# VectorE's order around the second group of scores, in an attention and MoE kernel on one core

## The chip, the cores and the metric

The kernel runs on one core of a Trainium2 chip. The metric is the device time of one execution in microseconds (us), and less is better. The engines are TensorE (PE, with its weight loads as PEld), VectorE (DVE), ScalarE (ACT), GpSimd (POOL) and SyncE (SP), which only issues transfers here.

## What is computed

The attention has B, H, S, D = 4, 8, 576, 64. Its output goes through a feed-forward layer of 512 by 2048, over 2304 tokens. All is float32.

```python
scores = q @ k^T / 8, causal mask, softmax            # per batch and head
local  = softmax @ v
mem    = (phi(q) @ M_prev) / (phi(q) @ z_prev + 1e-6) # phi(x) = max(x, 0) + min(exp(x), 1)
x      = g * mem + (1 - g) * local                    # g = sigmoid(beta), one per head
h      = x @ w_in
out    = (h * sigmoid(1.702 h)) @ w_out
```

## The kernel before

Two heads form a pair. There are 16 pairs, four per batch. Batch 0 goes another way (`plan_rest`) and is not touched. The twelve pairs of batches 1 to 3 are laid out by `plan_full`; here they are called pair 1 to pair 12. Beside them TensorE works off the first feed-forward layer, 1536 matmuls into `pm` (float32 split into high and low words, 12 matmuls to a block of 128 outputs). They serve as filling: `feed` and `step` put them between the pairs' own matmuls, and those that are left when the last pair is done run alone. Then 1008 matmuls into `acc` form the second layer.

A pair's 576 queries are four row blocks of 128, i = 0 to 3, and a tail of 64. A row block goes through five steps: scores on TensorE, maximum on VectorE (`max_unit`, line 649), exponential on ScalarE (`exp_unit`, L657), sum and reciprocal on VectorE (`inv_unit`, L745 and L746), scaling on GpSimd (`scale_unit`, L660). Then VectorE transposes it in 32 by 32 blocks into `eT` (`a_blocks`, L874). The tail does the same, and its blocks are set by `t_blocks` (L884). Beside that stand the memory term's steps: GpSimd's `qp` and `qmt` (L578, L169), VectorE's `norm` (L594 and L599, sum over `qmt` and its reciprocal), GpSimd's product of `qp` and `nrm`, and VectorE's `qblocks` (L617).

TensorE's stations in a pair are these: the second group (`second_group`), the scores of row blocks 2, 1 and 0 into the banks `rows`; `pm` matmuls; the next pair's tail scores and the first part of the values (`early_values`: 16 products `po<-qpt` and 36 `po<-eT`, which need the blocks of tail, third rows i = 3 and row block 2); `pm` matmuls; the second part (47 products, row block 1); the next pair's third-row scores; the third part (45 products, row block 0); `pm` matmuls. The banks of `rows` are those of `po`, so the next second group waits until `x_sums` and `x_rests` (ACT `xh`, DVE `xl`) have read the values.

VectorE also decodes a 64-bit-stored weight matrix in most pairs (`bit_ops`, L1124, L1125 and L1127, here called the raw words), after ScalarE's scaling of it (L1142). ScalarE empties the `pm` banks (`hk`, L161); there are two of them in this stage.

What sets the order: each step is entered with a slot and a priority (`at(slot, prio, fn)`). Within an engine a scheduler orders what is emitted, by priority and by its own picture of time. `tc.add_manual_dep` pins two instructions: NOSYNC fixes an order on one engine, SYNC makes one wait for another. `group` gives a run of matmuls one common wait at its first instruction, and TensorE works strictly in its order.

Of the kernel before, what the change touches and what calls it, by code (L numbers as in the profile page):

```python
# [12 lines left out]
ALU = mybir.AluOpType  # L13
# [27 lines left out]
def tile_attention_memory_moe(ctx, tc, kq, vq, mem, vt, qt, mt, zz, beta, w_in, w_out, out):  # L41
# [3 lines left out]
    STEP = 7  # L45
    PACE = ((36, 1.97), (67, 1.95), (9999, 2.3))
    LATE = 4
# [488 lines left out]
    def plan_prep(p):  # L536
# [54 lines left out]
        def norm():  # L591
            n = sml.tile([128, 9, 1], F32, name="nrm", bufs=2)
            P["n"] = n
            x = nc.vector.tensor_reduce(out=n[:, X:, 0], in_=qmt[:, X:9], op=ALU.add, axis=AX.X)  # L594
            if rest:
                behind_x(x)
            elif "tr" in state:
                tc.add_manual_dep(x.ins, state["max"], NOSYNC, reason="not yet")
            state["norm"] = nc.vector.reciprocal(out=n[:, X:], in_=n[:, X:]).ins.name  # L599
# [103 lines left out]

    def alone(p):
        names = rooms(KEEP)
        prep[p]["tail"] = [bank("ps") for _ in range(2)]
        group([lambda: s_tail(p, prep[p]["tail"])], names)
# [5 lines left out]
    def row_steps(p, U):  # L713
# [3 lines left out]
        def max_unit(h, i):  # L717
            n = 128 * (i + 1)
            U["nm", h, i] = softmax_max([(U["ps", h, i][:, :n], n, mask[:, 512 - n:])])
            state["max"] = last_max[0]  # L720
            if "qblocks" in P:
                tc.add_manual_dep(first_max[0], P["qblocks"], NOSYNC, reason="not yet")

# [19 lines left out]
        def inv_unit(i):  # L743
            sm = U["rs", i] = sml.tile([128, 2], F32, name="sm")
            nc.vector.tensor_reduce(out=sm, in_=U["sm", i], op=ALU.add, axis=AX.X)  # L745
            state["inv"] = nc.vector.reciprocal(out=sm, in_=sm).ins.name  # L746

# [113 lines left out]
    def plan_full(p):  # L861
# [19 lines left out]
        def t_blocks():  # L881
            e, a = blocks(), P["at"].rearrange("p (k n) -> p k n", n=32)
            for o, src in ((e[:, :, 4], a[:, :16]), (e[:, 4:6, 0], a[:, 16:])):
                x = nc.vector.transpose(out=o, in_=src)  # L884
                behind_x(x)
                if ("tr", 3) in P:
                    tc.add_manual_dep(x.ins, P["tr", 3], NOSYNC, reason="not yet")
            P["tr", 4] = x.ins.name
# [67 lines left out]
        def early_values():  # L956
# [3 lines left out]
            if p + 1 < len(pairs):  # L960
                names += rooms(0)
                prep[p + 1]["tail"] = [bank("ps") for _ in range(2)]
                fns.append(lambda: s_tail(p + 1, prep[p + 1]["tail"]))
            room()
# [4 lines left out]
        def first_group():  # L969
# [5 lines left out]
            group(fns, names)  # L975
            U["from"] = state["pe"]

        def second_group():
# [13 lines left out]
        tail_steps(p, TURN - 6 if p == MB * NP else K0[p - 1] + 7)  # L992
        at(k0 + 4, 89.5, t_blocks)
        at(k0, 20, first_group)
        at(k0 + 3, 18, lambda: feed(U["from"] + 2.9 - state["pe"]))
        at(k0 + 3, 20, second_group)
        at(k0 + 3, 22, lambda: feed(1.0, True))
        for i, k in ((3, 0), (2, 3), (1, 3), (0, 3)):
            x = k0 + k + 1
            for h in range(2):  # L1000
                at(k0 + k + 1, 13 - i, lambda h=h, i=i: max_unit(h, i))
                at(x, (30, 29, 26, 25)[i], lambda h=h, i=i: exp_unit(h, i))
                at(x + 1, 13 - i, lambda h=h, i=i: scale_unit(h, i))
            at(x, 91 - i, lambda i=i: inv_unit(i))
            at(k0 + (4 if i == 3 else 6), (18, 17, 16, 89.4)[i], lambda i=i: a_blocks(i))
        at(k0 + 7, 40, early_values)
        at(k0 + 7, 99, lambda: feed(1.0, True))
        if p + 1 == len(pairs):
            at(k0 + 8, 30, flush)
        at(k0 + 8, 32, x_sums)  # L1010
# [443 lines left out]
```

## Time and profile before

| what | us |
|---|---|
| median of 3 runs | 598.63 (598.5 to 598.97) |
| profiled execution | 596.94 |
| its span, first to last instruction | 595.1 |
| TensorE matmul busy in the span | 550.7 (93%) |
| VectorE busy | 424.4 (71%) |
| ScalarE busy | 342.0 (57%) |
| GpSimd busy | 245.4 (41%) |

The profiled execution is 1.84 us longer than its span and 1.69 us shorter than the median. Pair 1 starts its second group at 101.29 us, pair 12 at 323.61 us; the values of pair 12 end at 342.73 us, 516 `pm` matmuls follow until 414.98 us, and then the second layer. TensorE is the engine to read; from 342.73 us on it hardly waits. [...]

### The profile page before, as it was taken

To read this page: it belongs to the slowest core of one execution; us is meant where nothing else is said; L and a number is where in the kernel's file an instruction comes from. 1 tells how busy PE (TensorE), PEld (TensorE's weight loads), DVE (VectorE), ACT (ScalarE), POOL (GpSimd) and SP (SyncE) were. 2 spreads that over 40 slices of the span, in tenths; PEclk is the share of its full clock that TensorE was granted. 3 is DMA by queue.
4 is the path that set the end of the run, shared out by engine and by line. 5 is a ranking of instruction groups with operands and counts; after the bars stand their busy time and mean duration, and the time that the engine had idled before them with its cause. 6 is when DMAs were issued, how large, how long until landed. Compare 5 with 4: busy or idle time off the path is not lost.

```text
span 595.1 us, 17373 instructions
## 1 busy us (share of the span) xinstructions
PE 550.7 (93%) x6984; PEld 493.8 (83%) x6984; DVE 424.4 (71%) x994; ACT 342.0 (57%) x815; POOL 245.4 (41%) x326
## 2 busy tenths in 40 slices
PE   5699998978979899999989699999999999999997
PEld 3367766866858788887877699999999999999997
DVE  5878776667686777877686466786596768667964
ACT  5778876555446455655554236555766865676441
POOL 4858557664576367446645412310413201320000
PEclk8599999989989899999999889999999999999999
DMA  7986444446447645674455655232734804560002
GB/s 236 381 275 211 148 131 137 152 162 228 170 133 243 209 152 184 227 236 155 160 182 167 211 169 158 89 123 94 271 92 153 266 22 134 180 216 4 28 0 80
DMA packets 48736, 97.73 MB, mean 164 GB/s; under 512 B 5520, under 2 KB 33424, under 8 KB 48656
## 3 DMA queue, kind: packets, MB, share of 16 engines
q1 hardware_dynamic: 42416, 74.60, 37.4%
q0 software_dynamic: 6240, 22.02, 12.0%
q8 instruction: 55, 0.90, 0.6%
q14 instruction: 25, 0.20, 0.1%
HBM read 73.01 MB, written 23.59 MB: 162 GB/s over the span
## 4 chain that ended last, share of the span: by engine, by line
PE 75%; ACT 9%; DVE 7%; POOL 4%; issue 4%; DMA 1%; ACTq 0%; POOLq 0%; DVEq 0%
PE acc L1296 30%; PE pm L142 27%; PE po L142 9%; PE ps L142 4%; ACT a L657 3%; PE rows L142 3%; DVE ps L649 2%; POOL qmt L169 1%; DVE eT L874 1%; ACT qmt L563 1%; DVE r L1125 1%; POOL a L660 1%; ACT at L657 1%; DMA vr<-in_vq_dram 1%; ACT hk L161 1%
## 5 line engine op out<-in xcount | busy, mean ns | idle before, releaser
L142 PE MATMUL pm<-xh,wi 128*128 128x320 f32 (+1 forms) x1024 | 215.1, 303 | 7.0 <-ACT hk L161 5.5
L142 PEld LDWEIGHTS pm<-xh,wi 128*128 128x128 f32 x1024 | 165.8, 191 | 15.8 <-ACT hk L161 6.6
L1296 PE MATMUL acc<-oh,wo 128*128 128x384 f32 x672 | 169.6, 336 | 0.0
L142 PE MATMUL pm<-xl,wi 128*128 128x256 f32 (+1 forms) x512 | 151.5, 296 | 0.0
L1296 PEld LDWEIGHTS acc<-oh,wo 128*128 128x128 f32 x672 | 121.9, 188 | 0.0
L1296 PE MATMUL acc<-ol,wo 128*128 128x384 f32 x336 | 111.2, 337 | 0.0
L660 POOL TENSOR_SCALAR a<-a,sm,g 128x512 f32<-128x512 f32 (+3 forms) x112 | 69.2, 629 | 99.9 <-DVE sm L746 60.6
L169 DVE TENSOR_TENSOR ol<-g,oh 128x768 fp32r<-128x768 f32 x84 | 79.6, 954 | 43.0 <-ACT oh L161 42.8
L142 PEld LDWEIGHTS pm<-xl,wi 128*128 128x128 f32 x512 | 97.6, 191 | 0.0
L161 ACT ACTIVATE oh<-g 128x768 fp32r<-128x768 f32 x84 | 69.8, 842 | 45.9 <-PE acc L1296 36.0
L1239 POOL DMA_DIRECT2D g<-gd x48 | 34.8, 729 | 115.0 <-DVE ol L169 61.8
L161 ACT ACTIVATE hk<-pm 128x256 f32<-128x256 f32 (+1 forms) x112 | 44.7, 407 | 47.1 <-PE pm L142 37.7
L142 PEld LDWEIGHTS po<-eT,vr 32*64 32x64 f32 x3072 | 51.7, 135 | 17.9 <-issue 11.5
L1296 PEld LDWEIGHTS acc<-ol,wo 128*128 128x128 f32 x336 | 62.9, 188 | 0.0
L142 PE MATMUL po<-eT,vr 32*64 32x32 f32 (+4 forms) x3072 | 55.9, 256 | 6.2 <-issue 6.1
L142 PE MATMUL ps<-kqf 64*64 64x512 f32 (+3 forms) x288 | 38.3, 544 | 12.5 <-ACT qmt L570 5.1
L1245 ACT ACTIVATE g<-g 128x768 f32<-128x768 f32 x48 | 39.4, 839 | 15.4 <-DMA g<-gd 15.4
L169 DVE TENSOR_TENSOR g<-g,g 128x768 f32<-128x768 f32 x48 | 45.4, 951 | 1.4 <-ACT g L1245 1.4
L657 ACT ACTIVATE a<-rows,nm 128x256 f32<-128x256 f32 (+2 forms) x72 | 33.2, 474 | 20.3 <-DVE nm L649 20.3
L649 DVE CUSTOM_DVE_ANT_0 ps<-ps,mask 128x512 f32<-128x512 f32 (+3 forms) x72 | 38.0, 555 | 8.5 <-PE ps L142 7.8
L874 DVE STREAM_TRANSPOSE eT<-a 128x1024 f32<-128x1024 f32 (+3 forms) x48 | 39.5, 830 | 3.1 <-POOL a L660 2.1
L161 ACT ACTIVATE xh<-po 128x256 fp32r<-128x256 f32 (+2 forms) x54 | 14.2, 311 | 47.7 <-PE po L142 46.9
(145 smaller groups left out, 758.0 us busy)
## 6 DMA issues: line engine op xcount, KB each, us to landing
g<-gd POOLq DMA_DIRECT2D x48, 384.0 KB, 4.6
vr<-in_vt_dram SPq DMA_DIRECT2D x24, 576.0 KB, 4.8
gd<-hk SPq DMA_DIRECT2D x64, 160.0 KB, 3.0
kqf<-in_kq_dram SPq DMA_DIRECT2D x12, 768.0 KB, 5.4
wraw<-in_w_in_dram SPq DMA_DIRECT2D x16, 512.0 KB, 5.7
gd<-hk SPq DMA_DIRECT2D x64, 128.0 KB, 2.6
wraw<-in_w_out_dram SPq DMA_DIRECT2D x10, 512.0 KB, 4.8
qr<-in_qt_dram SPq DMA_DIRECT2D x12, 288.0 KB, 3.0
```

The lines of the kernel that those rows point to most:

```text
L142: x = nc.tensor.matmul(out, l, r, start=start, stop=stop)
L161: return nc.scalar.activation(out=dst, in_=src, func=AF.Copy, **kw)
L169: return (nc.vector if eng == "V" else nc.gpsimd).tensor_tensor(out=dst, in0=a, in1=b, op=op)
L563: x = nc.scalar.activation(out=qm, in_=qv(), func=AF.Relu, scale=-1.0)
L649: x = nc.vector.tensor_tensor_reduce(out=ps, in0=ps, in1=mk, op0=ALU.add, op1=ALU.min, scale=-0.125, scalar=1e38 if j == 0 else nm[:, j - ...
L657: return nc.scalar.activation(out=a, in_=ps, func=AF.Exp, scale=-1.0, bias=nm, accum_out=sm)
L660: return (nc.vector if eng == "V" else nc.gpsimd).tensor_scalar(out=a, in0=a, scalar1=r, scalar2=gcol, op0=ALU.mult, op1=ALU.mult)
L874: x = nc.vector.transpose(out=blocks()[:, :4 * i + 4, i:9 - i:8 - 2 * i].rearrange("p k h n -> p h k n"), in_=U["a", i].rearrange("p h (k ...
L1125: nc.vector.scalar_tensor_tensor(out=si, in0=raw[:, :, 1], scalar=-2 ** 31, in1=si, op0=ALU.bitwise_and, op1=ALU.bitwise_or)
L1239: x = nc.gpsimd.dma_start(t, gd[4 * kh + p][:, :, t0:t0 + QN].rearrange("i p t -> p i t"))
L1245: x = nc.scalar.activation(out=t, in_=t, func=AF.Gelu_apprx_sigmoid)
L1296: nc.tensor.matmul(acc[b, j][:, :QN], W[2 * p + kk][:, WPART[i], sp, 128 * j:128 * j + 128], mv[:, kk], start=first and p + kk == 0 and sp ...
```

## The change

It leaves all arithmetic as it is and sets orders and waits.

- `norm` gets an order behind the maximum emitted last (the next pair's third rows). Before, a condition that never held kept that out.
- `t_blocks` moves from behind the third rows' blocks to a place behind `qblocks`, and the second group's first maximum is ordered behind it.
- The reciprocal of row block 2 (U["inv", 2]) stands ahead of the maxima of row block 0; the sums of row blocks 1 and 0 stand behind row block 2's transposition.
- The next pair's tail scores form a group of their own (`alone(p + 1, 0)`), with their own wait; the wait for the blocks moves to the first product `po<-qpt`.
- In the last pair the second and third part of the values get `pm` matmuls between them (`last_values`).
- `PACE` rises from 2.3 to 2.45 for the late slots, and `feed` after the second group asks for 0.2 instead of 1.0. That moves filling between places.

```diff
-    PACE = ((36, 1.97), (67, 1.95), (9999, 2.3))
+    PACE = ((36, 1.97), (67, 1.95), (9999, 2.45))
...
-            elif "tr" in state:
+            else:
                 tc.add_manual_dep(x.ins, state["max"], NOSYNC, reason="not yet")
...
-    def alone(p):
-        names = rooms(KEEP)
+    def alone(p, keep=KEEP):
+        names = rooms(keep)
...
-            if "qblocks" in P:
-                tc.add_manual_dep(first_max[0], P["qblocks"], NOSYNC, reason="not yet")
+            if ("tr", 4) in P:
+                tc.add_manual_dep(first_max[0], P["tr", 4], NOSYNC, reason="not yet")
+            if i == 0 and ("inv", 2) in U:
+                tc.add_manual_dep(first_max[0], U["inv", 2], NOSYNC, reason="not yet")
...
-            nc.vector.tensor_reduce(out=sm, in_=U["sm", i], op=ALU.add, axis=AX.X)
-            state["inv"] = nc.vector.reciprocal(out=sm, in_=sm).ins.name
+            x = nc.vector.tensor_reduce(out=sm, in_=U["sm", i], op=ALU.add, axis=AX.X)
+            if i < 2 and ("tr", 2) in P:
+                tc.add_manual_dep(x.ins, P["tr", 2], NOSYNC, reason="not yet")
+            state["inv"] = U["inv", i] = nc.vector.reciprocal(out=sm, in_=sm).ins.name
...
-                behind_x(x)
-                if ("tr", 3) in P:
-                    tc.add_manual_dep(x.ins, P["tr", 3], NOSYNC, reason="not yet")
+                tc.add_manual_dep(x.ins, P["qblocks"], NOSYNC, reason="not yet")
...
-                names += rooms(0)
-                prep[p + 1]["tail"] = [bank("ps") for _ in range(2)]
-                fns.append(lambda: s_tail(p + 1, prep[p + 1]["tail"]))
+                alone(p + 1, 0)
...
+        def last_values():
+            late = values.pop("next")
+            group(late[1][:1], late[2])
+            feed(1.0, True)
+            group(late[1][1:], [])
...
-        at(k0 + 4, 89.5, t_blocks)
+        at(k0 + 2 + (p == MB * NP), 55, t_blocks)
...
-        at(k0 + 3, 22, lambda: feed(1.0, True))
+        at(k0 + 3, 22, lambda: feed(0.2, True))
...
-                at(k0 + k + 1, 13 - i, lambda h=h, i=i: max_unit(h, i))
+                at(x, (27.5, 12, 11, 10)[i], lambda h=h, i=i: max_unit(h, i))
-                at(x + 1, 13 - i, lambda h=h, i=i: scale_unit(h, i))
-            at(x, 91 - i, lambda i=i: inv_unit(i))
-            at(k0 + (4 if i == 3 else 6), (18, 17, 16, 89.4)[i], lambda i=i: a_blocks(i))
+                at(x + 1, (24, 23, 11, 10)[i], lambda h=h, i=i: scale_unit(h, i))
+            at(x + (i < 2), (22, 21, 27, 88)[i], lambda i=i: inv_unit(i))
+            at(k0 + (6, 6, 5, 4)[i], (18, 17, 16, 89.4)[i], lambda i=i: a_blocks(i))
...
-            at(k0 + 8, 30, flush)
+            at(k0 + 8, 30, last_values)
```

Three places show what that does to the engines' orders. The first is VectorE in pair 5, from the raw words to the next pair's `xl`; the two maxima of 128x512 are the third rows'. Before:

```order
L594 TENSOR_REDUCE nrm<-qmt 128x9
L599 RECIPROCAL nrm<-nrm 128x9
L1124 TENSOR_SCALAR r<-r 128x512
L1125 SCALAR_TENSOR_TENSOR r<-wraw,r 128x512
L1127 SCALAR_TENSOR_TENSOR r<-wraw,r 128x512
L649 ISA ps,nm<-ps,mask 128x512
L649 ISA nm 128x1
L649 ISA ps,nm<-ps,mask 128x512
```

After:

```order
L1130 TENSOR_SCALAR r<-r 128x512
L1131 SCALAR_TENSOR_TENSOR r<-wraw,r 128x512
L1133 SCALAR_TENSOR_TENSOR r<-wraw,r 128x512
L649 ISA ps,nm<-ps,mask 128x512
L649 ISA nm 128x1
L649 ISA ps,nm<-ps,mask 128x512
L649 ISA nm 128x1
L594 TENSOR_REDUCE nrm<-qmt 128x9
L599 RECIPROCAL nrm<-nrm 128x9
L169 TENSOR_TENSOR xl<-po,xh 128x256 x2
```

The norm has gone from the head of this run to behind the maxima, and so ahead of `xl` directly.

The second place is VectorE behind the maxima of the second group in pair 4 (`sum_167` belongs to row block 2; 2x16x32 is the third rows' transposition, 2x12x32 row block 2's). Before:

```order
L746 RECIPROCAL sm<-sm 128x2
L874 STREAM_TRANSPOSE eT<-a_2600 128x2x16x32
L884 STREAM_TRANSPOSE eT<-at 128x16x32
L884 STREAM_TRANSPOSE eT<-at 128x2x32
L745 TENSOR_REDUCE sm<-sum_168 128x2
L746 RECIPROCAL sm<-sm 128x2
L745 TENSOR_REDUCE sm<-sum_161 128x2
L746 RECIPROCAL sm<-sm 128x2
L874 STREAM_TRANSPOSE eT<-a_2691 128x2x12x32
```

After:

```order
L747 TENSOR_REDUCE sm<-sum_167 128x2
L750 RECIPROCAL sm<-sm 128x2
L649 ISA rows,nm<-rows,mask 128x128
L649 ISA nm 128x1
L649 ISA rows,nm<-rows,mask 128x128
L649 ISA nm 128x1
L878 STREAM_TRANSPOSE eT<-a_2584 128x2x16x32
L878 STREAM_TRANSPOSE eT<-a_2661 128x2x12x32
L747 TENSOR_REDUCE sm<-sum_168 128x2
L747 TENSOR_REDUCE sm<-sum_161 128x2
L750 RECIPROCAL sm<-sm 128x2 x2
```

Row block 2's blocks follow the third rows' directly; the tail's blocks and two sums with their reciprocals have left the place between.

The third place is TensorE at the early values of pair 2, printed with the waits of each instruction (the names after "waits" are semaphores of the engine or queue waited for; PE_49 and the like are counters of that engine). Before:

```order
L142 MATMUL ps<-kqf 64x256 [waits DMAHW4_49,DVE_49,Activation_49]
L142 MATMUL ps<-kqf 64x320
L142 MATMUL ps<-kqf 64x256
L142 MATMUL ps<-kqf 64x320
L142 MATMUL po<-qpt_1896,mr 64x160 [waits DMAHW2_49,PE_49]
L142 MATMUL po<-qpt_1896,mr 64x128
```

After:

```order
L142 MATMUL ps<-kqf 64x256 [waits DMAHW4_49]
L142 MATMUL ps<-kqf 64x320
L142 MATMUL ps<-kqf 64x256
L142 MATMUL ps<-kqf 64x320
L142 MATMUL po<-qpt_1896,mr 64x160 [waits DVE_49,DMAHW2_49,PE_49,Activation_49]
L142 MATMUL po<-qpt_1896,mr 64x128
```

The waits for VectorE and ScalarE have gone from the four tail scores to the first product behind them.

The numbers of `pm` matmuls at the three places of each pair (ahead of the early values, ahead of the second part, behind the third part), counted in TensorE's order:

| pair | before | after |
|---|---|---|
| 1 | 36, 12, 21 | 36, 12, 21 |
| 2 | 18, 9, 21 | 18, 9, 21 |
| 3 | 24, 15, 21 | 18, 9, 21 |
| 4 | 15, 0, 27 | 21, 6, 27 |
| 5 | 45, 12, 27 | 42, 15, 27 |
| 6 | 48, 9, 27 | 51, 18, 24 |
| 7 | 42, 15, 21 | 39, 9, 21 |
| 8 | 33, 18, 21 | 48, 15, 21 |
| 9 | 33, 18, 27 | 45, 18, 27 |
| 10 | 39, 18, 27 | 48, 9, 27 |
| 11 | 42, 15, 24 | 54, 15, 21 |
| 12 | 36, 12, then 516 alone | 42, 9, 12 ahead of the third part, then 468 alone |

## Rows read from the trace of the kernel before

**Rows 1.** Windows, pairs 2 to 11: length; busy PE, PEld, DVE, ACT, POOL; clock, DMA.

```profile
119.90:140.35 20.45, 17.32 (x381) 14.12 (x383) 12.80 (x44) 9.76 (x33) 11.54 (x15) 0.92 0.47 158
140.35:161.35 21.00, 18.87 (x392) 15.84 (x395) 14.87 (x46) 10.70 (x35) 11.54 (x15) 0.92 0.55 185
161.35:180.98 19.63, 15.58 (x374) 12.19 (x375) 15.91 (x46) 10.06 (x34) 12.99 (x16) 0.91 0.58 192
180.98:201.97 20.99, 18.76 (x413) 16.06 (x412) 14.84 (x46) 11.06 (x36) 10.98 (x16) 1.00 0.62 197
201.97:222.68 20.71, 20.50 (x417) 17.47 (x419) 14.97 (x46) 11.02 (x36) 11.53 (x15) 0.92 0.57 182
222.68:242.56 19.88, 19.88 (x410) 17.21 (x412) 15.17 (x47) 11.09 (x36) 11.63 (x15) 1.00 0.60 190
242.56:262.45 19.89, 19.08 (x405) 16.37 (x407) 15.01 (x46) 11.06 (x36) 11.62 (x15) 1.00 0.61 208
262.45:282.74 20.29, 19.02 (x410) 16.24 (x414) 14.95 (x46) 11.32 (x37) 11.97 (x16) 1.00 0.61 206
282.74:303.80 21.06, 18.68 (x416) 15.74 (x420) 14.84 (x46) 11.02 (x36) 11.32 (x16) 1.00 0.57 185
303.80:323.61 19.81, 18.59 (x410) 15.82 (x410) 13.97 (x44) 10.23 (x34) 12.10 (x16) 1.00 0.41 133
```

**Rows 2.** Waits of PE from 95 to 345 us: total, times, longest.

```profile
PE po L142 <- issue: 6.1, 4, 4.8
PE pm L142 <- ACT hk L161: 5.2, 4, 2.2
PE ps L142 <- ACT qmt L570: 5.1, 2, 3.0
```

**Rows 3.** Timeline of DVE, POOL and PE in pair 2: start, us, instruction, idle before.

```profile
120.83 0.57 DVE L649 CUSTOM_DVE_ANT_0 rows<-rows,mask 128x384 f32<-128x384 f32 x1 [0.92 <-PE rows L142]
...
123.34 0.16 DVE L746 RECIPROCAL sm<-sm 128x2 f32<-128x2 f32 x1
123.42 1.22 DVE L874 STREAM_TRANSPOSE eT<-a 128x1024 f32<-128x1024 f32 x1
...
124.57 0.80 DVE L884 STREAM_TRANSPOSE eT<-at 128x512 f32<-128x512 f32 x2
...
125.78 1.95 POOL L660 TENSOR_SCALAR a<-a,sm,g 128x256 f32<-128x256 f32 x4 [0.80 <-DVE sm L746]
...
126.21 1.99 DVE L874 STREAM_TRANSPOSE eT<-a 128x768 f32<-128x768 f32 x3
...
127.27 1.10 PE L142 MATMUL ps<-kqf 64*64 64x256 f32 x8 [3.01 <-ACT qmt L570]
```

**Rows 4.** Timeline of DVE and PE at the end of pair 5.

```profile
194.79 0.77 DVE L594 TENSOR_REDUCE nrm<-qmt 128x9 f32<-128x585 f32 x1 [2.94 <-POOL qmt L169]
...
198.29 0.69 DVE L649 CUSTOM_DVE_ANT_0 ps<-ps,mask 128x512 f32<-128x512 f32 x1
...
199.55 1.11 DVE L169 TENSOR_TENSOR xl<-po,xh 128x256 fp32r<-128x256 f32 x4
...
201.42 0.50 PE L142 MATMUL pm<-xh,wi 128*128 128x256 f32 x2 [2.23 <-ACT hk L161]
```

**Rows 5.** Timeline of DVE and POOL, end of pair 1 and middle of pair 2.

```profile
118.89 0.78 DVE L617 STREAM_TRANSPOSE qpt<-qp 128x576 f32<-128x576 f32 x1
...
127.69 1.65 POOL L578 TENSOR_SCALAR qp<-qr 128x576 f32<-128x576 f32 x1
...
132.80 0.77 DVE L594 TENSOR_REDUCE nrm<-qmt 128x9 f32<-128x585 f32 x1 [1.65 <-POOL qmt L169]
...
133.90 1.15 POOL L169 TENSOR_TENSOR qp<-qp,nrm 128x576 f32<-128x576 f32 x1 [0.21 <-DVE nrm L599]
```

**Rows 6.** The raw words' second step, by its line: duration least, median, most (ns).

```profile
L1125 DVE SCALAR_TENSOR_TENSOR r<-wraw,r x10: 692/1522/1648, 155.7 to 336.0; 128x512 int32<-128x512 int32 x10
```

**Rows 7.** The chain of waits in pair 6: start, us, what.

```profile
204.19 6.80 PE pm L142 x48
```

## The prediction

> **What bounds the kernel now.** I read four views in this order: busy time by windows, waits, timelines, chain. The change works in pairs 1 to 12. Pairs 2 to 11 last from 119.90 to 323.61 us, 203.7 us together [rows 1]. Length less PE busy gives TensorE's idle time in each: 3.1, 2.1, 4.1, 2.2, 0.2, 0, 0.8, 1.3, 2.4 and 1.2, together 17.4 us. Four pairs (2, 3, 4, 6) show a mean granted clock near 0.92 instead of 1.00, so part of each ran at the lower level: about 0.08 of 20.5, some 1.7 us each, 6.8 in all. Pair 12 has one gap more of 4.8 us ("issue") [rows 2]. So TensorE is the limit in most pairs, and in some it waits for a chain over the other engines.
>
> Two waits make up most of it. The first stands ahead of the early values: TensorE's tail scores stood 3.01 us in pair 2 [rows 3]. The wait is put down to ScalarE, but VectorE's last needed transposition (row block 2) began at 126.21 and TensorE went on at 127.27, so that is what ended last. Before that transposition VectorE did the third rows' blocks, the tail's blocks and the sums of two other row blocks [rows 3]. The second stands ahead of the second group: in pair 5 VectorE stood 2.94 us in the norm, for GpSimd's `qmt`, with the raw words and the third rows' maxima queued behind it. These maxima began at 198.29. ScalarE's exponentials wait for them, the emptying of `pm` banks stands behind those, and TensorE stood 2.23 us for a bank [rows 4]. Such bank waits sum to 5.2 us [rows 2].
>
> **The change part by part.** To load TensorE's pairs I take PE busy less the part lost to the clock: 15.7, 17.2, 13.8, 18.8, 18.8, 19.9, 19.1, 19.0, 18.7 and 18.6 for pairs 2 to 11 [rows 1]. A `pm` matmul costs 6.80 / 48 = 0.142 us [rows 7]. The table of the order moves matmuls by 0, -12, +12, 0, +9, -9, +12, +12, 0, +9, so the new loads are 15.7, 15.5, 15.5, 18.8, 20.1, 18.6, 20.8, 20.7, 18.7, 19.9. That is 33 matmuls more (4.7 us); they no longer run alone at the end.
>
> Row block 2's blocks: in pair 2 the third rows' transposition ends at 124.57, when the tail's begins. GpSimd's scaling of row block 2 ended at 125.78 - 0.80 = 124.98, and its reciprocal (123.34) now stands ahead of two maxima, which brings that to some 124.6 [rows 3]. So the transposition can begin at 124.7 instead of 126.21, and TensorE is let go 1.5 us earlier, 5.9 us after the second group's start instead of 7.4. The tail scores (1.10 us at the lower clock) no longer wait for it and fill the gap's first part. Of 3.01 us about 0.5 are left, and with them goes, I take it, the drop of the clock.
>
> The norm and the tail's blocks: they lengthen another chain, the round from one row block 2 to the next, which I sum from the rows of before. Sums, reciprocals and, in pairs 2 and 3, a tail maximum that now stands ahead of them: 0.84 (125.37 to 126.21), some 1.2 with the maximum. GpSimd's scaling of row blocks 1 and 0: 1.95, now behind row block 2's transposition. From there to the norm 132.80 - 127.69 = 5.1 [rows 5]; the tail's scaling, which lay beside the norm, now stands mostly ahead of it, so up to 0.8 more: 5.9. Norm to the end of GpSimd's product: 133.90 + 1.15 - 132.80 = 2.25. `qblocks` 0.78, tail blocks 0.80, the third rows' sum about 0.3: 1.9. Maxima to the third rows' transposition 123.42 - 120.83 = 2.6, that one 1.15, row block 2's to TensorE's start 1.06: 4.8. The sum is 18.0, with gaps 18.1 us a round [rows 3, 5]. No pair can be shorter than its round, except pair 2, which follows pair 1 without lag: 5.9 + 1.2 + 1.95 + 5.9 to the norm, 1.0 for it and 1.11 for `xl` [rows 4, 5] make 17.1, when the banks for the next second group are free.
>
> The raw words now stand ahead of third rows' maxima and norm, in a time in which GpSimd works on `qp` and `qmt`. Between the norm's end (195.8 with its reciprocal) and the maxima at 198.29 they took 2.5 us [rows 4]; their second step took 1.52 us in the median and 0.69 at the least [rows 6]. If they end before `qmt` does, they add nothing to the round (18.1); if they end last, they add up to their 2.5 less some slack, 2.1, giving 20.2. I take a third, 18.8 us, since ScalarE's input for them comes soon after the tail's exponentials. [...]
>
> The sum: pair 2 takes 17.1; pairs 3, 4, 5, 7 and 10 take 18.8 each (94.0); pairs 6, 8, 9 and 11 take their loads, 20.1 + 20.8 + 20.7 + 19.9 = 81.5. Together 192.6. Pair 1 gets 0.7 more, since the tail's blocks (0.80) now stand ahead of its `xl`. Of the bank waits I keep half, 2.6, since second groups' maxima come up to 2 us late in a round-bound pair and ScalarE's emptying is queued behind their exponentials; the bounds are 0 and 5.2 [rows 2]. That makes 195.9 against 203.7: 7.8 us saved.
>
> Pair 12: 12 `pm` matmuls, 1.7 us, go between second and third part, where the 4.8 us gap lay. I let that gap shrink by them alone; it can stay whole (0) or vanish (4.8, and some clock). Nothing in the rows shows what TensorE waited for. [...]
>
> All: 7.8 + 4.7 + 1.7 = 14.2 us. The profiled execution (596.94, span 595.1) would come to 582.7; the median stands 1.69 above it, so the forecast is 598.63 - 14.2 = **584.4 us**. `PACE` and `feed` cost nothing beyond the matmuls that they move, and the pairs of batch 0 nothing: the same matmuls run there in the same order.
>
> **The rivals.**
> First, the round stays at 18.1 and the bank waits vanish. Then pairs 3 to 5, 7 and 10 take 18.1, 18.1, 18.8, 18.6 and 18.7, the sum with pairs 2, 6, 8, 9 and 11 and pair 1's 0.7 is 191.6, and 12.1 + 4.7 + 1.7 = 18.5 are saved: 580.1 us. For it: those maxima come early wherever ScalarE's input is early. Against: GpSimd stands in the round.
> Second, the raw words end last, and the round is 20.2. Pairs 3 to 7, 10 and 11 take 20.2, and 17.1 + 141.4 + 20.8 + 20.7 + 0.7 + 2.6 = 203.3; 0.4 + 4.7 + 1.7 = 6.8 are saved: 591.8 us. For it: the 1.52 us of rows 6.
> Third, fewer matmuls are left alone at the end, 48 times 0.142 = 6.8 us, and what is prepared under them (second layer's weights) may need that time. Then these 6.8 are given back: 591.2 us. Against: TensorE showed no wait there, and VectorE's share is 71% over the whole.
> Fourth, slower. The norm now holds `xl`, and `xl` holds the banks of the next second group, so TensorE would wait for GpSimd's `qmt` in every pair. At a round of 22 us pairs 3 to 11 take 198.0, with 17.1 and 0.7 that is 215.8, 12.1 more than before; less 4.7 and 1.7 the time is 604.3. It decides from a round of (203.7 + 6.4 - 17.8) / 9 = 21.4 on, 3.3 above my sum. Against: the pairs of before lasted 20.4 on average with waits that the new order takes out.
> Fifth, it doesn't do what it says: the wait ahead of the early values ends with ScalarE, which the view names, and other stalls come back. Then only the tail scores' own time is won and the matmuls moved cover little, within 1 us of 598.6.
>
> **How the numbers follow.** Chances: forecast 0.45, first rival 0.22, second 0.17, third 0.06, slower 0.05, no effect 0.05. The likeliest case alone covers 581 to 588 (bank waits 0 to 5.2, gap of pair 12). The range takes in the first rival with pair 12's gap half gone (577) and the second and third with a little more (593). Differences within 0.2% (1.2 us) can't be told from none. Faster comes to 0.90, no change to 0.05, slower to 0.05.
>
> **What would show it.** The wait of tail scores for VectorE or ScalarE should be gone from TensorE's waits, with a gap of some 0.5 to 2 us ahead of `po<-qpt` instead, largest in pairs 3 and 4. VectorE should no longer stand 2.9 us in the norm, and the third rows' maxima in pair 5 should begin some 2 us earlier after its second group. Granted clock should be 1.00 in pairs 2 and 6. Pairs 3 and 4 should last 18 to 19 us; at 20 or more the raw words or GpSimd's chain set the round, to be seen in the duration of the second raw-word step and in the norm's wait. If the `acc` phase begins later than 68 us after the last values, or shows gaps, the third rival holds. A bound I left out would show as equal lengths of light and heavy pairs above 20.5 us.

## Result and the profile after

The changed kernel takes 581.6 us in the median (580.6 to 582.6, 4 runs), the kernel before beside it 598.8 us. The ratio is 0.9713 with the interval [0.9692, 0.9733]. 17.2 us are saved; the forecast was 14.2 and the range held the time. The profiled execution of the changed kernel took 580.95 us with a span of 579.2, 15.9 less than the span before.

The busy time by windows, cut at the starts of the second groups of pairs 2 to 12 and at the end of the last values; columns are the stretch in us, its length, TensorE's busy time (instructions), the granted clock, the DMA share and GB/s:

```profile
120.70:137.77 17.07, 15.80 (x378) 1.00 0.48 155
137.77:155.91 18.14, 15.59 (x377) 1.00 0.58 205
155.91:174.68 18.77, 16.46 (x383) 1.00 0.58 200
174.68:194.44 19.76, 19.01 (x413) 1.00 0.67 228
194.44:214.91 20.47, 20.47 (x423) 1.00 0.64 210
...
295.78:316.42 20.64, 20.58 (x420) 1.00 0.39 130
316.42:333.47 17.05, 16.75 (x377) 1.00 0.77 252
```

Pairs 2 to 11 last 316.42 - 120.70 = 195.7 us instead of 203.7 [rows 1], although 33 `pm` matmuls more run in them. The clock is 1.00 in every pair; before it was near 0.92 in four of them. Pair 12 takes 17.05 us instead of 19.1. The matmuls alone behind it take 64.2 us (333.5 to 397.7) instead of some 72.

TensorE's waits from 95 to 345 us (what stood, for what; us in total, times, the longest):

```profile
PE po L142 <- DVE sm L747: 3.1, 3, 1.3
PE rows L142 <- DVE xl L169: 2.8, 2, 1.5
PE pm L142 <- ACT hk L161: 2.1, 6, 0.5
PE po L142 <- issue: 1.3, 4, 0.6
PE pm L142 <- DVE xl L169: 0.8, 1, 0.8
```

The tail scores (`ps`) wait for nothing any more; what is left of that wait stands ahead of `po`. The "issue" gap of 4.8 us [rows 2] has gone. In pair 5, where VectorE had stood 2.94 us in the norm with the third rows' maxima behind it [rows 4], VectorE now does this:

```profile
187.47 1.12 DVE L1130 TENSOR_SCALAR r<-r 128x512 int32<-128x512 int32 x1 [1.68 <-ACT r L1148]
188.63 0.69 DVE L1131 SCALAR_TENSOR_TENSOR r<-wraw,r 128x512 int32<-128x512 int32 x1
189.35 0.69 DVE L1133 SCALAR_TENSOR_TENSOR r<-wraw,r 128x512 int32<-128x512 int32 x1
189.97 0.69 DVE L649 CUSTOM_DVE_ANT_0 ps<-ps,mask 128x512 f32<-128x512 f32 x1
...
191.23 0.75 DVE L594 TENSOR_REDUCE nrm<-qmt 128x9 f32<-128x585 f32 x1
```

The maxima begin 15.3 us after the pair's second group (189.97 - 174.68), before it was 17.3, and the norm finds `qmt` ready. So the signs that the prediction named are there, but for one: the gaps ahead of `po<-qpt` are 0.97, 1.27 and 0.81 us in pairs 2, 3 and 4, so pair 4's is not among the largest. What the profile cannot say is which of the edits brought it about: the change has six parts, and several of them could have removed the same idle time.

### The profile page after: what moved, and what is told of

Same layout as the page of the kernel before. It is cut to its first block, busy times and chain, and to the rows that moved or that the text cites. A ratio compares the mean times of both kernels' runs of the same rounds, so it can differ in the third digit from the quotient of the medians.

```text
span 579.2 us, 17363 instructions
## 1 busy us (share of the span) xinstructions
PE 546.8 (94%) x6984; PEld 488.1 (84%) x6984; DVE 423.7 (73%) x993; ACT 343.4 (59%) x816; POOL 249.0 (43%) x326
## 4 chain that ended last, share of the span: by engine, by line
PE 72%; ACT 9%; DVE 8%; POOL 4%; issue 3%; DMA 2%; SPq 0%; POOLq 0%; ACTq 0%; DVEq 0%
PE acc L1302 30%; PE pm L142 26%; PE po L142 8%; PE ps L142 4%; ACT a L657 4%; PE rows L142 2%; DMA gd<-hk 2%; DVE ps L649 2%; ACT hk L161 1%; POOL qp L169 1%; DVE eT L878 1%; POOL qmt L169 1%; ACT xh L161 1%; ACT mr L161 1%; PE pt L153 1%
## 5 line engine op out<-in xcount | busy, mean ns | idle before, releaser
L142 PEld LDWEIGHTS pm<-xh,wi 128*128 128x128 f32 x1024 | 163.6, 189 | 15.0 <-ACT hk L161 5.5
L142 PEld LDWEIGHTS po<-eT,vr 32*64 32x64 f32 x3072 | 49.9, 130 | 13.6 <-issue 5.1
L142 PE MATMUL po<-eT,vr 32*64 32x32 f32 (+4 forms) x3072 | 54.6, 250 | 1.3 <-issue 1.3
L142 PE MATMUL ps<-kqf 64*64 64x512 f32 (+3 forms) x288 | 37.1, 531 | 2.0 <-ACT ec L161 1.1
L161 ACT ACTIVATE xh<-po 128x256 fp32r<-128x256 f32 (+2 forms) x54 | 14.2, 311 | 41.2 <-PE po L142 40.3
```

Source lines behind the costliest of these rows:

```text
L142: x = nc.tensor.matmul(out, l, r, start=start, stop=stop)
L161: return nc.scalar.activation(out=dst, in_=src, func=AF.Copy, **kw)
```

## Experiments

Each kernel is the changed one with a part undone, or the one before with a part alone; the last four (e7, e8, e11, e12) go on from the changed kernel or from e2. To compare them I use two numbers of each profiled execution: the stage from the second group of pair 1 to the first `acc` matmul, and in it the idle time, which is the sum of what the timeline gives as idle ahead of TensorE's instructions. The stage less the idle time is time in which matmuls run; in the changed kernel, whose granted clock is 1.00 in the whole stage, it is 287.0 us, and what a kernel has well above that goes with stretches at the lower clock (before, e1 and e9, with 291.1 to 292.3, have five, two and two pairs at a mean of 0.88 to 0.92). It is no sharp measure: e3, at 1.00 throughout as well, has 285.6. Executions of one kernel lie 2 to 6 us apart, so a difference of 1.5 us between medians of different kernels says little.

| kernel | median us | ratio to before | stage | idle | stage less idle |
|---|---|---|---|---|---|
| before | 598.8 | 1 | 313.5 | 22.1 | 291.4 |
| changed | 581.6 | 0.971 [0.969, 0.973] | 295.6 | 8.6 | 287.0 |
| changed, norm in front again (e1) | 593.2 | 0.991 [0.988, 0.994] | 307.1 | 16.0 | 291.1 |
| changed, old order of blocks (e2) | 580.2 | 0.969 [0.966, 0.972] | 294.9 | 8.0 | 286.9 |
| changed, tail scores in the group (e3) | 581.4 | 0.971 [0.969, 0.973] | 296.7 | 11.1 | 285.6 |
| changed, last values in one group (e4) | 583.8 | 0.974 [0.971, 0.977] | 299.7 | 10.9 | 288.8 |
| before, norm behind (e5) | 591.7 | 0.988 [0.983, 0.992] | 307.8 | 18.5 | 289.3 |
| before, new pacing (e6) | 582.3 | 0.974 [0.970, 0.977] | 300.2 | 12.6 | 287.6 |
| before, VectorE's whole new order (e9) | 592.3 | 0.987 [0.984, 0.991] | 308.6 | 16.2 | 292.3 |
| before, new pacing and norm behind (e10) | 582.9 | 0.974 [0.971, 0.976] | 298.1 | 11.4 | 286.7 |

The profiled executions of e4, e6 and e9 stand 1.6, 2.7 and 1.5 us above their medians, those of before and e2 1.9 and 1.2 below.

### The norm in front again

```diff
-            else:
+            elif "tr" in state:
                 tc.add_manual_dep(x.ins, state["max"], NOSYNC, reason="not yet")
```

> The changed kernel with one line undone: the norm of the next pair stands again ahead of the raw words and the third rows' maxima. TensorE's order is that of the changed kernel to the instruction. Theory (the norm's place matters): VectorE stands in the norm for GpSimd's `qmt` again, some 1 to 2 us a pair in which it now waits 0.1; the third rows' maxima begin 2 to 3 us later after the second group, and TensorE's waits for `pm` banks grow from 2.1 us to 5 or more. The round itself is no longer, so the time rises by 3 to 5 us only: 584.5 to 586.5 us, ratio to the changed kernel 1.005 to 1.009. Rival (VectorE only waits elsewhere, ScalarE's input of the raw words holds the maxima in any case): within 1 us of 581.6.

It took 593.2 us, 11.6 above the changed kernel: the theory had the direction and a third of the size. The price is in pairs 3 to 5, which take 20.90, 22.18 and 22.50 us (together 8.9 more than in the changed kernel). VectorE in pair 4, timeline (start, us, operation, idle ahead of it):

```profile
174.17 0.76 DVE L594 TENSOR_REDUCE nrm<-qmt 128x9 f32<-128x585 f32 x1 [4.97 <-POOL qmt L169]
...
175.50 1.53 DVE L1131 SCALAR_TENSOR_TENSOR r<-wraw,r 128x512 int32<-128x512 int32 x1
177.06 0.69 DVE L1133 SCALAR_TENSOR_TENSOR r<-wraw,r 128x512 int32<-128x512 int32 x1
177.67 0.69 DVE L649 CUSTOM_DVE_ANT_0 ps<-ps,mask 128x512 f32<-128x512 f32 x1
...
178.93 1.12 DVE L169 TENSOR_TENSOR xl<-po,xh 128x256 fp32r<-128x256 f32 x4
```

VectorE stands 4.97 us in the norm, and the raw words, the third rows' maxima and `xl` come behind it. `xl` holds the banks that TensorE needs, so TensorE stands too, 3.38 us, and then works at a granted clock of 0.50. Its timeline in pair 4, and the windows around that stand:

```profile
179.40 0.74 PE L142 MATMUL pm<-xl,wi 128*128 128x256 f32 x2 [3.38 <-DVE xl L169]
181.75 2.84 PE L142 MATMUL rows<-kqf 64*64 64x384 f32 x24
```

```profile
179.40:181.75 2.35, 1.68 (x6) 0.52 0.67 197
181.75:185.00 3.25, 3.25 (x27) 0.50 0.68 220
```

The 24 `rows` matmuls of a second group, which took 1.53 us in pair 6 of this run at 1.00, took 2.84. So the theory's "The round itself is no longer" was wrong: with the norm in front, all that is queued behind it on VectorE joins the round over GpSimd.

### The old order of blocks and sums

```diff
-        at(k0 + 2 + (p == MB * NP), 55, t_blocks)
+        at(k0 + 4, 89.5, t_blocks)
...
-            at(x + (i < 2), (22, 21, 27, 88)[i], lambda i=i: inv_unit(i))
+            at(x, 91 - i, lambda i=i: inv_unit(i))
```

(and with these the priorities and "not yet" rules of maxima, sums and transpositions that the change had altered)

> The changed kernel with VectorE's order in the first half of a pair undone: tail blocks behind the third rows' blocks, the third rows' reciprocal and that of row block 2 behind the maxima. Norm, tail scores, `PACE` and TensorE's whole order stay as changed. Theory (TensorE is let go by row block 2's transposition): it comes 1.5 us later again, the early values' first matmul waits 1.5 us longer in each of the pairs 2 to 5 and 7 to 11 that had a gap or next to none, and the granted clock falls in two or three pairs: plus 6 to 10 us, 587.5 to 591.5 us. Rival (the tail scores' own wait and the moved matmuls carry the gain): within 2 us of 581.6.

580.2 us: the rival. The early values' first matmul does go out later after the second group, 6.9 to 7.2 us instead of 6.0 to 7.0 in pairs 2 to 4, in pair 4 with this wait:

```profile
163.59 0.77 PE L142 MATMUL po<-qpt,mr 32*64 32x160 f32 x30 [1.65 <-ACT qmt L570]
```

But what counts is the round from one such matmul to the next. From pair 1 to pair 5 the four rounds take 17.84 + 18.86 + 17.87 + 18.61 = 73.2 us here, and 16.98 + 17.36 + 18.78 + 19.85 = 73.0 in the changed kernel. Putting the tail's blocks (0.80) ahead takes them out of the piece between maxima and release, and puts them into the piece between GpSimd's product and the maxima, which belongs to the same round.

### The tail scores in the group again

```diff
-                alone(p + 1, 0)
+                names += rooms(0)
+                prep[p + 1]["tail"] = [bank("ps") for _ in range(2)]
+                fns.append(lambda: s_tail(p + 1, prep[p + 1]["tail"]))
```

> The changed kernel with the tail scores waiting for the early values' whole group again. The pacing then moves matmuls too: 507 of `pm` instead of 531 are left after the last values. Theory: in the light pairs (2, 3, 4, 7, 10) the 1.1 us of the tail scores stand behind the wait instead of in it, so TensorE is let go as before and ends 1 us later there, plus 4 us in these, and 24 matmuls (3.4 us) fill other gaps or only move: 583 to 586 us. Rival (the wait is so short by now that the scores' place is worth nothing, and fewer matmuls are left): 578 to 581 us.

581.4 us, the same as the changed kernel, between theory and rival. Waits ahead of the tail scores are back (three, together 5.1 us), and 24 matmuls less are left at the end. As far as the spread of the runs lets one tell, the one pays for the other.

### The last pair's values in one group

```diff
-            at(k0 + 8, 30, last_values)
+            at(k0 + 8, 30, flush)
```

> The changed kernel with the last pair's second and third part of the values in one group again, no matmuls of `pm` between (480 instead of 468 behind them). All else as changed. Theory (the 4.8 us without a releaser come from the run of short matmuls): TensorE's gap in pair 12 is back with 4 to 5 us, and the time rises to 585.5 to 586.5 us. Rival (the gap came from what the DMA engines did at that moment in the kernel before, and is gone with the times shifted): the gap stays under 0.5 us, and the time at 581 to 582 us.

583.8 us, 2.2 more; the intervals of the two ratios overlap. The gap is back with 2.73 us, not 4 to 5 as the theory had it and not under 0.5 either, and the clock falls to 0.50 behind it:

```profile
332.27 1.92 PE L142 MATMUL po<-eT,vr 32*64 32x160 f32 x48 [2.73 <-issue]
```

```profile
332.27:336.00 3.73, 3.73 (x55) 0.50 0.40 142
336.00:340.00 4.00, 4.00 (x20) 0.61 0.72 239
```

### One part alone on the kernel before

The norm's place alone is the edit of the first experiment made on the kernel before, the other way round:

> The kernel before with one line changed: the norm of the next pair stands behind the third rows' maxima, as in the changed kernel. Everything else as before, TensorE's order too. Theory (after the run that put the norm back and lost 11.6 us: a norm in front makes raw words and third rows' maxima part of the round over GpSimd): most of the gain comes from this line, 588 to 591 us, the lengths of pairs 3 to 5 fall below 19.5 us, and the clock drops of pairs 2 to 6 become fewer. Rival (the norm costs so much only where tail blocks and sums are in the new order; in the old one TensorE waits for row block 2's blocks in any case): 594 to 597 us, and the tail scores' wait of 2 to 3 us stays in the light pairs.

591.7 us: 7.2 us are saved, just above the theory's end. Pairs 2 to 11 take 197.0 us (120.34 to 317.32) instead of 203.7, with the same matmuls; the waits of the tail scores stay, and so does pair 12's gap, with 4.68 us.

The pacing alone:

```diff
-    PACE = ((36, 1.97), (67, 1.95), (9999, 2.3))
+    PACE = ((36, 1.97), (67, 1.95), (9999, 2.45))
...
-        at(k0 + 3, 22, lambda: feed(1.0, True))
+        at(k0 + 3, 22, lambda: feed(0.2, True))
...
-            at(k0 + 8, 30, flush)
+            at(k0 + 8, 30, last_values)
```

> The kernel before with the pacing of the changed one (`PACE` 2.45, `feed(0.2)`, the last pair's values in two parts with a block of `pm` between): 57 `pm` matmuls more run beside the pairs, VectorE's order stays as before. Theory (they fill TensorE's idle time in the light pairs and pair 12's gap): 57 times 0.142 is 8.1 us less alone, less what the heavier pairs, bound by TensorE, pay for theirs (half, 4 us), and 2 to 4 us of pair 12's gap: 590 to 593 us. Rival (the pairs take longer by what is added, since each bank filled more must be emptied by ScalarE behind the exponentials): 596 to 599 us.

582.3 us, with VectorE's old order. That is 16.5 us saved, far outside what the theory gave it, and within the measurement's reach of the whole change. Here are its pairs 2 to 6, as windows:

```profile
120.80:140.12 19.32, 16.94 (x378) 0.91 0.50 162
140.12:160.25 20.13, 17.39 (x389) 1.00 0.62 204
160.25:180.08 19.83, 16.65 (x371) 0.83 0.56 169
180.08:202.07 21.99, 20.42 (x425) 1.00 0.62 206
202.07:221.93 19.86, 19.86 (x419) 1.00 0.61 186
```

Pairs 2 to 11 last 203.1 us (120.80 to 323.94), as long as before, and hold 57 matmuls more. These 57, some 8 us by the 0.142 us of [rows 7], came for nothing, where the theory let half of them be paid for. Pair 12 takes 16.2 us instead of 19.1, without a gap. The clock drops of pairs 2 and 4 stay. The edit has three parts, which were not separated; for the last pair's split alone there is only the 2.2 us of e4, in the changed kernel.

VectorE's whole new order with the old pacing is the changed kernel with `PACE`, `feed`, `flush` and the tail scores' group put back; its diff is the sum of those above:

> The changed kernel's whole order of VectorE (norm behind the maxima, tail blocks in front, third rows' reciprocal early) with the old pacing: `PACE` 2.3, `feed(1.0)`, the last pair's values in one group, the tail scores in the early values' group. TensorE's order is that of the kernel before, with 564 `pm` matmuls alone at the end. Theory (the pacing carries the gain; the order adds nothing to the norm's place, which alone gave 591.7): 589 to 593 us. Rival (the steps of the prediction: the order lets the early values go 1.5 us sooner and takes the clock drops away, 7.8 us in the pairs beside the matmuls moved): 584 to 588 us.

592.3 us, as the theory had it: no better than the norm alone. In its profile pairs 2 to 11 are as short as 194.0 us (120.09 to 314.11), 3.0 less than with the norm alone, but behind them the gap of pair 12 (4.76 us) and the lower clock (0.50 for 3.84 us) are there, and a wait of 2.0 us among the matmuls alone. Its runs lie between 588.3 and 593.8, so a gain of the order over the norm alone, of up to 3 us, is not excluded. Last, pacing and norm together, on the kernel before:

> The kernel before with the new pacing and the norm behind the maxima, but the old order of blocks and sums and the tail scores in their group. Theory (what the norm's place saved in TensorE's idle time is mostly filled by the pacing's matmuls, so both do the same work once): 579.5 to 582.5 us, against 582.3 for the pacing alone. Rival (the two add up, 16.5 and 7.2 us): 574 to 577 us.

582.9 us: no better than the pacing alone, 0.4 above the theory's end and far from the rival. 16.5 and 7.2 do not add up; both remove the same idle time of TensorE (12.6 us of it are left with the pacing alone, 11.4 with both).

### GpSimd's round, the raw words, and more pacing

In the changed kernel GpSimd's `qp<-qr` gets a step of its own, `qrelu`, that waits only for the scaling of row block 2:

```diff
+            x = nc.gpsimd.tensor_scalar(out=qp[:, X:9], in0=qv(), scalar1=0.0, scalar2=None, op0=ALU.max)
+            if "scaled2" in state:
+                tc.add_manual_dep(x.ins, state["scaled2"], NOSYNC, reason="not yet")
...
+            at(s0 + 5, 24.5, qrelu)
```

> The changed kernel, and GpSimd's `qp<-qr` (1.65 us a pair) put between the scaling of row block 2 and that of row blocks 1 and 0, where GpSimd stood 1.4 us for reciprocals, instead of behind the latter. Theory (the round over GpSimd sets pairs 3 to 5, 7 and 10): GpSimd's chain from the scaling to the norm gets 1.4 us shorter, pairs 3 to 5 and 10 shrink by 0.7 to 1.4 us each down to their load on TensorE: 576 to 579 us. Rival (VectorE's raw words and its waits for ScalarE set the round): within 1 us of 581.6, with the norm then waiting for nothing.

582.3 us (e7, ratio 0.973 [0.969, 0.977]): the rival's time, in its bounds. Pairs 3 and 4 take 17.46 and 18.03 us, 0.7 less each, and the norm waits for nothing. VectorE in pair 4, then GpSimd:

```profile
166.11 2.12 DVE L1141 TENSOR_SCALAR r<-r 128x512 int32<-128x512 int32 x1 [0.88 <-ACT r L1159]
...
169.60 0.69 DVE L656 CUSTOM_DVE_ANT_0 ps<-ps,mask 128x512 f32<-128x512 f32 x1
...
170.86 0.75 DVE L600 TENSOR_REDUCE nrm<-qmt 128x9 f32<-128x585 f32 x1
```

```profile
166.57 2.56 POOL L169 TENSOR_TENSOR qmt<-qp,zb 128x512 f32<-128x512 f32 x3
172.01 1.15 POOL L169 TENSOR_TENSOR qp<-qp,nrm 128x576 f32<-128x576 f32 x1 [2.88 <-DVE nrm L605]
```

`qmt` is ready at 169.13, but the norm comes at 170.86, behind raw words and maxima. So in these pairs two chains of nearly the same length set the round, GpSimd's and VectorE's over the raw words, and shortening one by 1.4 us gives 0.7. In the profiled execution more than this is given back in pair 6 (23.8 us instead of 20.5), with a gap of 1.69 us ("issue") in the third part of the values and a mean clock of 0.93 over the pair.

The raw words taken out of the changed kernel, a kernel that leaves out the decoding of ten blocks of the second layer's weights:

```diff
-        at(state["slot"] + 5, 57, bits)
```

> The changed kernel without VectorE's raw-word steps in the pairs (three instructions for each of 10 blocks of the second layer's weights are left out, so these weights are not put together; their loads and ScalarE's step stay). Theory (they lengthen the round, since GpSimd's `at`, `qp` and `qmt` took 5.1 us beside them in pair 4 and 4.1 us in pair 2 without): pairs 4, 5, 7 and 10 shrink by 0.7 to 1.2 us: 577.5 to 579.5 us. Rival (they lie in VectorE's wait for the third rows' scores and for `qmt` and cost nothing): 581 to 582 us.

577.7 us (e8, 0.964 [0.960, 0.968]), 3.9 less, the theory's time, but of its pairs (4, 5, 7 and 10) only pair 4 has a part in it: pair 3 takes 16.78 instead of 18.14 us and pair 4 17.54 instead of 18.77, while 5, 7, 10 and the others change by about 0.3 at most. Since the raw words cost something in so few places, I put them elsewhere, in the kernel of the second experiment:

```diff
-    for i in range(2 * len(HERE)):
-        at(K0[MB * NP + 2 + i] + 3, 58, lambda i=i: decode(i))
+    for i, (j, k) in enumerate(((5, 3), (6, 3), (6, 5), (8, 3), (8, 5), (9, 3), (9, 5), (11, 3), (11, 5), (12, 3))):
+        at(K0[MB * NP + j - 1] + k, 58, lambda i=i: decode(i))
```

> The kernel of the second run (changed, with the old order of blocks and sums, 580.2 us), and the ten blocks of raw words placed in other pairs: none in pairs 3, 4, 7 and 10, whose length the round sets, two each in pairs 6, 8, 9 and 11, where TensorE is never idle, one each in 5 and 12. Theory (without any raw words the changed kernel took 577.7, 3.9 us less, and that is lost in the light pairs): 576.5 to 578.5 us. Rival (VectorE has no slack in the heavy pairs either; two blocks there hold up the next maxima and TensorE waits for banks): 580 to 584 us.

585.1 us (e11, 0.978 [0.975, 0.981]), 4.9 above the second experiment: the rival and somewhat more. Pairs 3 and 4 do get shorter, by 0.3 and 0.6 us (17.38, 17.69), but pairs 7, 9, 10 and 12 get 1.2, 1.6, 1.1 and 1.4 longer (20.03, 22.60, 20.22, 19.00). These follow the pairs with two blocks, and VectorE's timeline at the start of pair 9 shows why:

```profile
256.78 1.14 DVE L1131 SCALAR_TENSOR_TENSOR r<-wraw,r 128x512 int32<-128x512 int32 x1
257.95 0.57 DVE L649 CUSTOM_DVE_ANT_0 rows<-rows,mask 128x384 f32<-128x384 f32 x1
```

The second block fell ahead of the row maxima of the next second group, which began at 255.70; they come 2.3 us behind it, where in pair 6 of the same kernel it is 0.9 (195.55 after 194.62). So this run shows what a block costs in that place. Whether the heavy pairs have slack at another place, it does not tell, and that stays open.

More pacing, in the kernel of the second experiment too:

```diff
-    PACE = ((36, 1.97), (67, 1.95), (9999, 2.45))
+    PACE = ((36, 1.97), (67, 1.95), (9999, 2.70))
```

> The kernel of the second run (580.2 us) with `PACE` 2.70 instead of 2.45: 447 `pm` matmuls alone at the end instead of 531, 84 more beside the pairs, all of them in pairs 6 to 10; pairs 2 to 5 get none, since the inputs of further matmuls are not there yet. Theory (a matmul that is moved gains only where TensorE would be idle; what idle time is left, 8 us, lies mostly in pairs 2 to 5): 578.5 to 581.5 us, the heavy pairs longer by what the end gets shorter. Rival (each one moved gains its 0.142 us, as from 2.3 to 2.45, where 57 moved with the last pair's split gave 16 us): 568 to 572 us.

587.6 us (e12, 0.982 [0.979, 0.986]), 7.3 above the second experiment and worse than either expected. Its windows for pair 12, the matmuls alone, and the start of `acc`; then TensorE's and ScalarE's timeline there:

```profile
326.80:346.07 19.27, 16.38 (x377) 1.00 0.69 227
346.07:397.30 51.23, 51.23 (x386) 1.00 0.44 144
397.30:410.00 12.70, 8.21 (x37) 0.87 0.47 155
```

```profile
406.40 1.53 PE L1300 MATMUL acc<-oh,wo 128*128 128x384 f32 x4 [4.36 <-ACT oh L161]
```

```profile
400.74 1.06 ACT L161 ACTIVATE wo<-st 128x1024 fp32r<-128x1024 f32 x1 [0.22 <-DVE st L169]
404.56 1.06 ACT L161 ACTIVATE wo<-st 128x1024 fp32r<-128x1024 f32 x1 [2.75 <-DVE st L169]
405.52 2.29 ACT L161 ACTIVATE oh<-g 128x768 fp32r<-128x768 f32 x3
```

The matmuls alone end at 397.3 us (396.3 in the second experiment, 397.7 in the changed kernel), so moving 84 more won nothing in the pairs, as the theory had it. But only 51 us of them are left, and the second layer's weights (`st`, `wo`), which VectorE and ScalarE prepare in that time, are not done: `acc` stands 4.36 us for `oh`, which is queued behind `wo` on ScalarE. From there to the end it is 186.9 us instead of 181.5. This is the prediction's third rival. It does not decide at the change's 531 matmuls, but at 447 it does. In pair 12 "issue" gaps of 1.56 and 1.33 us stand besides, since no `pm` matmuls are left between the second and the third part of the values there.

## Why the prediction was right, and where it was not

**The sum by stages held, in part by luck.** The 195.9 us forecast had pair 1's 0.7 in it. So pairs 2 to 11 were 195.2 us forecast and 195.7 measured, and pair 1's second group begins 0.8 us later, behind its tail blocks. Pair 2: 17.1 and 17.07. Pairs 3, 4, 5, 7 and 10: 94.0 and 18.14 + 18.77 + 19.76 + 18.85 + 19.93 = 95.5. Pairs 6, 8, 9 and 11, taken as TensorE's loads: 81.5 and 20.47 + 21.08 + 21.01 + 20.64 = 83.2. Together the pairs are 3.1 us over, and the 2.6 us that I had added for bank waits makes up for most of it (the waits for ScalarE's `hk` measured 2.1). The round sets pairs 3 and 4 alone. In pairs 5, 7 and 10 TensorE is busy for 19.01 of 19.76, 18.85 of 18.85 and 18.97 of 19.93 us, and without the raw words (e8) they take 19.71, 18.57 and 20.21; that 18.8 each came out near is their load (18.8, 18.6 and 18.7 in the prediction), not the round. The 33 matmuls were 4.7 us forecast; with 64.2 us for 468 of them, 0.137 each, they made 4.5.

**The mis-sized term is pair 12's gap.** I let it shrink by the 1.7 us of the matmuls put into it, with 0 and 4.8 "and some clock" as bounds. From pair 12's second group to `acc` the profile shows 414.8 - 323.6 = 91.2 us before and 397.7 - 316.4 = 81.3 after, 9.9 less; the matmuls make 4.5 of that, so the gap and what hung on it were worth 5.4. The gap alone is 4.82 - 0.24 = 4.6. The remaining 0.8 fits the lower clock behind it, which I had not priced. That the gap shrinks by the matmuls put into it was the wrong step: they split a long run of short matmuls, and with it the gap goes (last section). In the timeline and the windows of the kernel before the gap and the clock are to be seen:

```profile
334.31 2.95 PE L142 MATMUL po<-eT,vr 32*64 32x128 f32 x170
342.07 0.66 PE L142 MATMUL po<-eT,vr 32*64 32x32 f32 x14 [4.82 <-issue]
```

```profile
337.00:342.07 5.07, 0.26 (x12) 0.72 0.71 251
342.07:346.00 3.93, 3.93 (x26) 0.50 0.33 86
346.00:350.00 4.00, 4.00 (x29) 1.00 0.42 162
```

After 4.8 us of standing TensorE worked at a granted clock of 0.50 for 3.9 us. With 8.0 in pairs 2 to 11, 8.0 + 4.5 + 5.4 is 17.9 us, which is what the stage became shorter (313.5 to 295.6). The spans differ by 2.0 us less, 15.9, since the stage begins 0.8 later and `acc` takes 181.5 us instead of 180.3. The medians differ by 17.2, as the profiled execution of before lies 1.9 us below the median measured beside the change, that of the changed kernel 0.7 below its own.

**The step on row block 2's blocks was right in place and worth nothing.** TensorE is let go 6.0 us after pair 2's second group (5.9 forecast). But without that order the rounds are as long, and the kernel as fast (e2). I had both halves of this, 1.5 us won ahead of the release and 1.9 us of blocks and sums in the round, and did not set the one against the other.

**The clock drops went, but not by that step.** In the trace of the kernel before, the granted clock stands at 1.00 or at 0.50: each of the four pairs has 3.41 us at 0.50 (from 127.57, 148.05, 168.53 and 202.66 us on), half of which is the 1.7 us that I had taken from the means. I tied the drops to the tail scores that fill the wait. With the tail scores in the group again (e3) the granted clock is 1.00 in the whole stage. With the old order (e2) one drop is left, in pair 2 (mean 0.91); with the pacing alone (e6) two are, in pairs 2 and 4 (0.91 and 0.83); with VectorE's new order and the old pacing (e9) two as well, in the same pairs (0.91 each), beside pair 12's and one among the matmuls alone (a mean of 0.66 from 365 to 370 us). So the order and the pacing each have a part in it, and no run separates which step takes which drop. Where the clock is at 0.50 in the rows above, TensorE had stood just before, 3.38 us in e1, 2.73 in e4, 4.82 in the kernel before. But not every stand brings a drop: in e3 TensorE stands 2.99 us in pair 4, at 1.00.

**The step on the norm was right for this kernel and for a stronger reason.** I gave it the bank waits. In the new order it keeps raw words, maxima and `xl` out of GpSimd's round: undone, it costs 11.6 us, which is the mechanism of the fourth rival, at 22 us in pairs 4 and 5. In the old order with the new pacing it is worth nothing that can be told (582.3 and 582.9). A reason for that can be read in one place: in pair 4 of e6 the raw words stand ahead of the norm in any case, and VectorE waits 0.53 us for `qmt` there, against 4.97 us in e1:

```profile
173.97 0.77 DVE L594 TENSOR_REDUCE nrm<-qmt 128x9 f32<-128x585 f32 x1 [0.53 <-POOL qmt L169]
```

For the other pairs it stays open.

**The raw words** cost more than I took. Without them pairs 3 and 4 take 16.8 and 17.5 us, where I had 18.1, and with them 18.1 and 18.8: 1.3 us each, not 0.7. Two errors cancelled. The second rival's mechanism is real, its full price (20.2) is not reached.

**`PACE` was booked wrongly.** I wrote that `PACE` and `feed` cost nothing beyond the matmuls they move, and counted these as a gain of 4.7 us beside the pairs' 7.8, which I gave to VectorE. The runs show one stock of idle time, 22 us before. Shortening the pairs with the same matmuls (e9: pairs 9.7 us shorter) or filling them at the same length (e6: 57 more in 203.1 us) draws on it in two ways, and who does both gets it once. The pacing with the last pair's split gets nearly all of it alone; VectorE's order does not: from pair 12's second group to `acc` e9 takes 96.0 us, against 91.2 before and 81.3 in the changed kernel, with the gap of 4.8 us as it was, a further wait of 2.0 and more time at the lower clock (0.50 to 0.68 from 332.16 to 340 us, 0.66 from 365 to 370). That the stages added up was no evidence for the parts.

No kernel that does the whole work beats the changed one by more than the runs' spread: e2, with only norm, pacing and tail scores changed, took 580.2 against 581.6, and the intervals of the two ratios overlap.

## What to carry to other kernels

Where a change hands out idle time of the engine that bounds, add up stages, not edits: parts that each remove the same idle time look worth 16 and 7 us alone and are worth 16 together. Before reordering another engine, try whether the bound engine's own spare work, put into its gaps, does the same; it does so until the work left for later no longer covers what is prepared beneath it. And a step that is moved ahead of a release must be followed once round the whole loop, since in a cycle it only changes the piece in which it stands.

## What the runs showed of the hardware

The gap without a releaser in pair 12 comes and goes with how the short matmuls stand. Where the last two parts of the values run as one group, it is 4.82 us (before), 4.68 (e5), 4.76 (e9) and 2.73 (e4), and in e12, whose pacing leaves no `pm` between them, two gaps of 1.56 and 1.33. Where 12 long `pm` matmuls stand between them at the pacing of 2.45, it is 0.84 us at the most in the nine kernels that have them (changed, e1, e2, e3, e6, e7, e8, e10, e11). In the kernel before TensorE goes through 170 short matmuls in 2.95 us right ahead of the gap; split in two, the pieces are of some 90, as 94 in 1.48 us in the changed kernel. The waits view names no releaser, but the trace also records the packets of a DMA queue that the page lists under "instruction", q8: 55 packets of 16 KB each in the kernel before. Late in the changed kernel, from 414 to 549 us, TensorE starts 240 to 276 matmuls and weight loads from one packet to the next. In the kernel before such a packet runs from 339.54 to 340.58 us, inside the gap, and TensorE goes on 1.49 us behind its end. All eight stands that the traces of the kernel before and of the changed one put down to "issue" between 100 and 420 us, 0.21 to 4.82 us long, end 1.3 to 1.6 us behind the end of a q8 packet. My reading of these times is that TensorE waits there for instructions; no view names that as the cause. Of the 85 q8 packets of the two traces in that stretch 77 have no such stand behind them. The one behind the run of 170 short matmuls has it: 4.8 us, and 3.9 us at a granted clock of 0.50 behind it, as in e9:

```profile
327.00:332.16 5.16, 0.40 (x23) 0.96 0.80 278
332.16:336.00 3.84, 3.84 (x26) 0.50 0.34 82
336.00:340.00 4.00, 4.00 (x21) 0.68 0.46 169
```

VectorE's first raw-word step, with one input, took 0.37 us in e1's pair 4, from 175.10 us on, where GpSimd stood until 175.33, and 2.12 us in e7's, beside `at` and `qmt` on GpSimd. In the changed kernel it took 0.43 us in pair 4, beside `at`, and 1.12 in pair 5, beside `qmt`. So it varies as the second step does (0.69 to 1.65 us [rows 6]), for which alone I had given two durations; what draws it out no run separates.
